# Float32 attention premix in four array quarters and postmix in two halves, two groups of rows at a time

## Chip, cores, metric

One core of a Trainium2 chip runs the whole program in one launch. The metric is the time of one execution in microseconds of the device; the median of the runs counts. The array's clock has two levels, 1.2 and 2.4 GHz; the profile gives the granted share of the higher one.

## What is computed

Twelve-head attention over two batches of 448 rows (head size 64) with two mixing matrices between the heads, then two pairs of dense layers on its 896 x 768 result:

```
scores = scale * matmul(q, k.T)
scores = einsum('bhij,hg->bgij', scores, w_pre)
attn = softmax(scores, axis=-1)        # sum + 1e-09 below
attn = einsum('bhij,hg->bgij', attn, w_post)
x = matmul(attn, v)                    # to 896 x 768
x = moe(x, w_in, w_out)                # h * clip(h + 3, 0, 6) / 6 between
out = moe2(x, w_in, w_out, a, b)       # a cubic over a quadratic in h between
```

All inputs are float32 (the layer weights arrive as 64-bit words whose halves the kernel puts together).

## The kernel before

The kernel has an attention stage and a stage of the dense layers. This case is about the first.

**Chunks and groups.** `plan` cuts each batch's 448 query rows into four chunks, of 120, 120, 120 and 88 rows. A chunk is cut into groups of GR = 10 rows: 12, 12, 12 and 9 of them, 90 in all (m = 0 to 89). For one group the 10 rows times 12 heads are laid on 120 partitions, so that mixing the heads is one product with a 120 x 120 block-diagonal matrix.

**Scores.** `scores(C, hp)` makes the scores of two heads of a chunk: three float32r products (high times high, low times high, high times low) of 64 rows each, one head in the upper and one in the lower 64 rows of the array, into two PSUM banks `sc`. Two copies (L273), one on ScalarE and one on VectorE, move the banks to a staging tile, and DMAs on SP's queue (`spread`, L251) lay it out over the partitions of `full[C]` by row and head. There are two `full` buffers: chunk C+1 is filled while chunk C is used. `k_prep` and `q_prep` split k and q into a high and a low float32r part, the high one on ScalarE and the low one on VectorE.

**A group.** `gsplit` (L293, L295, on GpSimd) splits a group of `full` into `sh` and `sl`. `premix` (L305 to L307) runs three float32r products over the whole array into a bank `M`, VectorE takes the row maximum (L309), ScalarE the exponent with its sum (L311). `norm` (L319, L320) makes the reciprocal of the sum on VectorE, `weigh` (L324, ScalarE) multiplies the block-diagonal postmix matrix `wq` by it into `wr`. `postmix` (L340) has four float32 products, one for each 112 of the 448 columns, with `e` as weights and `wr` as the moving operand, into a bank `A`; an evacuation (L347, some on VectorE) puts it into `at`. The postmix of group m - 2 stands behind the premix of group m. A float32 product appears in the trace as two records, each with a weight load of its own.

**Values.** `av_unit` (L362) multiplies `at` by v for two heads of a chunk, eight float32 products of 64 output columns that alternate between the left and the right half of the array, into a bank `X`; `av_evac` splits the result into the float32r input of the dense layers.

**The order** is written by hand in the loop over chunks and groups: a step is one group; the score pairs of the next chunk stand at steps 1, 3, 5 (two pairs each; 0, 2, 4 in a chunk of 9 groups), the value units of the chunk before at steps 7, 9, 11 (5, 7, 8). Chunk 0 has no value units, and its first scores and those of half of chunk 1 are made ahead of it. In the last chunk (7) the steps also carry the first pieces of the dense layers' weights: `to_f32` on ScalarE and VectorE (L434 to L442) and the split `wh`, `wl` on GpSimd (L458, L459), and the first products `h`.

**PSUM.** Eight banks: two `M`, two `A`, four `sc` (which also serve `X`).

Of the kernel before, what the change touches and what calls it, by code (L numbers as in the profile page):

```python
# [7 lines left out]
F32 = mybir.dt.float32  # L8
# [13 lines left out]
GR = 10  # L22
# [24 lines left out]

@with_exitstack
def fused_kernel(
# [30 lines left out]
    wp_h = const.tile([GP, GR, H], F32R, name="wp_h")  # L80
    wp_l = const.tile([GP, GR, H], F32R, name="wp_l")
    wq = const.tile([GP, H, GR], F32, name="wq")
    mask = const.tile([GP, GR], F32, name="mask")
    wrep = const.tile([GP, 2, H], F32, name="wrep")
# [10 lines left out]
    PRE2 = list(range(2, 12))  # L95
    dram = ctx.enter_context(tc.tile_pool(name="dram", bufs=1, space=bass.MemoryType.DRAM))
# [8 lines left out]
    wtmp = front.tile([GP, GR, H], F32, name="wtmp")  # L105
# [32 lines left out]
    def load_vs():  # L138

        C = len(chunks) - 1  # L140
        t = att.tile([JP, NP, 2, JC * D], F32, tag="full", bufs=2, name="vlast")
# [8 lines left out]
    pw = ps.tile([128, 512], F32, tag="A", name="warm_ps")  # L150
# [9 lines left out]
    for i, w in enumerate((w_pre, w_post)):  # L160
        nc.sync.dma_start(
            out=wrep[:, i, :], in_=w[None, :, :].to_broadcast([GR, H, H])
        )
    load_q(1)
    nc.scalar.preload_act_table_set("natural_log_exp_and_others")
    nc.gpsimd.memset(mask, 1.0)
    nc.gpsimd.affine_select(out=mask, in_=mask, pattern=[[-H, GR]], compare_op=ALU.is_ge,
                            fill=0.0, base=0, channel_multiplier=1)
    nc.gpsimd.affine_select(out=mask, in_=mask, pattern=[[H, GR]], compare_op=ALU.is_ge,
                            fill=0.0, base=H - 1, channel_multiplier=-1)  # L170
# [13 lines left out]
    def build_mix():  # L184
        nc.gpsimd.tensor_tensor(
            out=wtmp,
            in0=mask[:, :, None].to_broadcast([GP, GR, H]),
            in1=wrep[:, 0, None, :].to_broadcast([GP, GR, H]),
            op=ALU.mult,
        )  # L190
        nc.gpsimd.tensor_scalar(out=wtmp, in0=wtmp, scalar1=float(D) ** -0.5, scalar2=None, op0=ALU.mult)
# [805 lines left out]
```

## Time and profile before

| what | value |
|---|---|
| median of 3 runs | 707.35 us (706.45 to 708.13) |
| profiled execution, its own time | 706.12 us |
| span of the profiled execution | 704.4 us |
| granted clock of the array | 0.999 of full speed |
| PE busy | 692.8 us, 98% of the span |
| PEld (weight loads) busy | 618.4 us, 88% |
| DVE (VectorE) busy | 557.1 us, 79% |
| ACT (ScalarE) busy | 411.4 us, 58% |
| POOL (GpSimd) busy | 257.2 us, 37% |
| DMA | 122.81 MB, mean 174 GB/s |

Times in the rows are microseconds from the span's start unless marked ns. A matmul's record begins when it is dispatched and ends when its result stands in PSUM, so records of neighbours overlap: what a matmul costs the array is the distance from one record's start to the next one's, and not its length. The first record after a pause includes the load of its weights. A row marked "x8" merges eight instructions that follow each other.

### The profile page before, as it was taken

To read this page: it belongs to the slowest core of one execution; us is meant where nothing else is said; L and a number is where in the kernel's file an instruction comes from. 1 tells how busy PE (TensorE), PEld (TensorE's weight loads), DVE (VectorE), ACT (ScalarE), POOL (GpSimd) and SP (SyncE) were. 2 spreads that over 40 slices of the span, in tenths; PEclk is the share of its full clock that TensorE was granted. 3 is DMA by queue.
4 is the path that set the end of the run, shared out by engine and by line. 5 is a ranking of instruction groups with operands and counts; after the bars stand their busy time and mean duration, and the time that the engine had idled before them with its cause. 6 is when DMAs were issued, how large, how long until landed. Compare 5 with 4: busy or idle time off the path is not lost.

```text
span 704.4 us, 12410 instructions
## 1 busy us (share of the span) xinstructions
PE 692.8 (98%) x4461; PEld 618.4 (88%) x4461; DVE 557.1 (79%) x934; ACT 411.4 (58%) x851; POOL 257.2 (37%) x255
## 2 busy tenths in 40 slices
PE   8999999999999999999999999999999999999997
PEld 4779888888889888889888888888999999999997
DVE  6855585665567699989998777879999889989991
ACT  6777787787887434434422221247766667669851
POOL 2886775887776333432344454400000000000000
PEclk9999999999999999999999999999999999999999
DMA  6646476545393544454355555367666474755522
GB/s 200 231 135 175 150 202 196 155 140 169 118 262 110 169 130 147 141 169 147 127 171 163 166 187 161 100 241 269 204 243 218 169 264 158 241 184 202 190 80 89
DMA packets 76033, 122.81 MB, mean 174 GB/s; under 512 B 6805, under 2 KB 56261, under 8 KB 75973
## 3 DMA queue, kind: packets, MB, share of 16 engines
q1 hardware_dynamic: 75684, 121.66, 54.2%
q8 instruction: 35, 0.57, 0.3%
q10 hardware_dynamic: 288, 0.37, 0.1%
q14 instruction: 26, 0.20, 0.1%
HBM read 83.39 MB, written 19.27 MB: 146 GB/s over the span
## 4 chain that ended last, share of the span: by engine, by line
PE 60%; DVE 26%; DMA 5%; issue 4%; ACT 3%; POOL 0%; ACTq 0%; POOLq 0%; DVEq 0%
PE A L340 9%; DVE wf L438 6%; DVE wf L442 6%; PE h L388 6%; PE h L387 6%; PE h L386 6%; PE acc L388 6%; PE acc L386 6%; PE acc L387 6%; PE X L362 5%; PE sc L270 4%; DMA pre<-wf 4%; DVE gl L565 4%; DVE wf L436 3%; PE M L305 3%
## 5 line engine op out<-in xcount | busy, mean ns | idle before, releaser
L388 PE MATMUL h<-xh,wl 128*128 128x512 f32 (+1 forms) x384 | 140.7, 366 | 0.9 <-DVE wl L462 0.9
L386 PE MATMUL h<-xh,wh 128*128 128x512 f32 (+1 forms) x384 | 141.1, 367 | 0.0
L387 PE MATMUL h<-xl,wh 128*128 128x512 f32 (+1 forms) x384 | 140.7, 366 | 0.0
L434 ACT ACTIVATE wf<-wraw 128x768 f32<-128x768 f32 (+1 forms) x56 | 48.8, 881 | 92.9 <-DMA pre<-wf 55.1
L295 POOL TENSOR_TENSOR sl<-full,sh 120x448 fp32r<-120x448 f32 x87 | 100.1, 1151 | 7.3
L309 DVE TENSOR_REDUCE st<-M 120x1 f32<-120x448 f32 x90 | 56.0, 623 | 51.1 <-PE M L307 50.6
L340 PEld LDWEIGHTS A<-wr,e 120*112 120x112 f32 x720 | 86.4, 176 | 8.1 <-ACT wr L324 4.0
L340 PE MATMUL A<-wr,e 120*112 120x120 f32 x720 | 88.9, 266 | 2.2 <-ACT wr L324 2.2
L458 POOL TENSOR_SCALAR wh<-wf 128x768 fp32r<-128x768 f32 (+1 forms) x34 | 32.6, 959 | 139.5 <-DVE wf L442 134.8
L311 ACT ACTIVATE e<-M,st 120x448 f32<-120x448 f32 x90 | 57.2, 635 | 40.5 <-DVE st L309 35.4
L388 PEld LDWEIGHTS h<-xh,wl 128*128 128x128 f32 x384 | 72.2, 188 | 9.8 <-DVE wl L462 1.2
L386 PEld LDWEIGHTS h<-xh,wh 128*128 128x128 f32 x384 | 72.2, 188 | 8.0
L387 PEld LDWEIGHTS h<-xl,wh 128*128 128x128 f32 x384 | 72.2, 188 | 7.8
L388 PE MATMUL y<-gh,wl 128*128 128x384 f32 x192 | 70.8, 369 | 0.1
L386 PE MATMUL y<-gh,wh 128*128 128x384 f32 x192 | 70.5, 367 | 0.0
L293 POOL TENSOR_SCALAR sh<-full 120x448 fp32r<-120x448 f32 x87 | 53.9, 619 | 44.0 <-PE M L306 19.5
L387 PE MATMUL y<-gl,wh 128*128 128x384 f32 x192 | 69.9, 364 | 0.0
L459 POOL TENSOR_TENSOR wl<-wf,wh 128x768 fp32r<-128x768 f32 (+1 forms) x34 | 67.7, 1992 | 2.8
L438 DVE SCALAR_TENSOR_TENSOR wf<-wraw,icst,wf 128x768 int32<-128x768 int32 (+1 forms) x56 | 61.7, 1103 | 0.7
L436 DVE TENSOR_SCALAR wf<-wf 128x768 int32<-128x768 int32 x66 | 42.5, 644 | 21.8 <-ACT wf L434 21.5
L442 DVE SCALAR_TENSOR_TENSOR wf<-wraw,icst,wf 128x768 int32<-128x768 int32 (+1 forms) x56 | 57.7, 1032 | 0.6
L564 ACT ACTIVATE gh<-g 128x384 fp32r<-128x384 f32 (+1 forms) x32 | 18.6, 580 | 60.5 <-DVE g L562 60.2
(114 smaller groups left out, 1522.2 us busy)
## 6 DMA issues: line engine op xcount, KB each, us to landing
wraw<-in_moe_w_out_dram SPq DMA_DIRECT2D x28, 768.0 KB
wraw<-in_moe_w_in_dram SPq DMA_DIRECT2D x22, 768.0 KB
full<-stg SPq DMA_DIRECT2D x60, 210.0 KB
vraw<-in_v_dram SPq DMA_DIRECT2D x42, 224.0 KB
wpre<-in_moe_w_in_dram SPq DMA_DIRECT2D x10, 768.0 KB
w2h<-wh SPq DMA_DIRECT2D x16, 384.0 KB
w2l<-wl SPq DMA_DIRECT2D x16, 384.0 KB
ws<-w2h SPq DMA_DIRECT2D x16, 384.0 KB
```

The costliest lines, as they stand in the source:

```text
L293: eng.tensor_scalar(out=sh[:r], in0=s[:r], scalar1=1.0, scalar2=0.0, op0=ALU.mult, op1=ALU.add)
L295: return lambda: eng.tensor_tensor(out=sl[:r], in0=s[:r], in1=sh[:r].bitcast(F32), op=ALU.subtract)
L309: nc.vector.tensor_reduce(out=st[:r, 0:1], in_=mt[:r, :S], op=ALU.max, axis=AX.X, negate=True)
L311: nc.scalar.activation(out=e[:r], in_=mt[:r, :S], func=AF.Exp, bias=st[:r, 0:1], accum_out=st[:r, 1:2])
L340: nc.tensor.matmul(av[:, jc], lhsT=e[:r, jc * JP : (jc + 1) * JP], rhs=wr[:r, :, :rr], start=True, stop=True)
L386: nc.tensor.matmul(o, lhsT=wh, rhs=mh, start=first, stop=False)
L387: nc.tensor.matmul(o, lhsT=wh, rhs=ml, start=False, stop=False)
L388: nc.tensor.matmul(o, lhsT=wl, rhs=mh, start=False, stop=last)
L436: nc.vector.tensor_scalar(out=wi, in0=wi, scalar1=3, scalar2=None, op0=ALU.logical_shift_left)
L438: nc.vector.scalar_tensor_tensor(out=wi, in0=hw, scalar=icst[:, 0:1], in1=wi, op0=ALU.bitwise_and, op1=ALU.bitwise_or)
L442: nc.vector.scalar_tensor_tensor(out=wi, in0=lw, scalar=icst[:, 1:2], in1=wi, op0=ALU.logical_shift_right, op1=ALU.bitwise_or)
L459: nc.gpsimd.tensor_tensor(out=lv, in0=w, in1=hv.bitcast(F32), op=ALU.subtract)
```

## The change

It touches the attention stage alone; the dense layers are the same.

Groups of chunks 1 to 7 are taken two at a time: a chunk of 12 groups has 6 steps, one of 9 has 5, the last of them with a single group. `full` has 128 partitions, and a head of a group row lies at partition 13 i + h (`part_of`; one that would fall on 128 lies at 64), so that five rows of a group lie in either half of 64 partitions; the unused partitions are zeroed once. The premix of two groups is four float32 products of 64 x 64 (`wph` in both halves): half x of the rows, and column half i for group i, into bank `M[x]`. The split on GpSimd (`gsplit`) is gone. The exponents of bank x hold five rows of both groups. The postmix (L357) takes partitions 0 to 59 for the first group and 64 to 123 for the second: 16 float32 products of 60 rows and 60 columns for two groups, in alternation in the upper and the lower half of the array, into two banks `A`. A single group in these chunks has one float32 premix of 128 rows (`wpf`), and chunk 0 keeps groups one at a time on 120 partitions, with one float32 premix (L306).

PSUM is now four `M`, two `A`, two `sc`. `weigh` runs on GpSimd (L319), and the normalization and the weights of a step's groups are made at the start of the next step, ahead of the premix. Both copies of a score pair are on VectorE (L276). The low parts of q (from chunk 3 on) and of the second batch's k are on GpSimd. A step has up to two places for units, "a" right behind the premix and "b" behind the postmix: score pairs at 0a, 0b, 1a, 1b, 2a, 2b in a chunk of 6 steps (0a, 0b, 1a, 1b, 2a, 3a of 5), value units at "b" of the last three steps, two in each. The postmix is that of two steps before; in the last chunk that of one step before, and there each step advances the weight pieces twice. The mixing matrices come laid out from the host side and are loaded instead of being built.

The core of the diff:

```diff
+HR = GR // 2
+HS = H + 1
+NQ = HR * H
+
+
+def part_of(i, h):
+
+    p = HS * i + h
+    return p if p < 128 else 64
...
+    BUFS = {"M": 4, "A": 2, "sc": 2}
...
+    full = [att.tile([128, MG, S], F32, tag=f"full{i}", bufs=1, name=f"full{i}") for i in range(2)] * NCH
+    nc.gpsimd.memset(full[1], 0.0)
...
+    def scores(C, hp, tags=("sc", "sc"), st=None, first=nc.vector.tensor_copy,
                second=nc.vector.tensor_copy):
...
+    def soft_max(e, x):
+        n, st, mt = e["n"], e["st"], e["M"][x]
+        nc.vector.tensor_reduce(out=st[:n, x : x + 1], in_=mt[:n, :S], op=ALU.max, axis=AX.X, negate=True)
+        t = att.tile([128, S], F32, tag="e", bufs=6, name=f"e{e['id']}_{x}")
+        nc.scalar.activation(out=t[:n], in_=mt[:n, :S], func=AF.Exp, bias=st[:n, x : x + 1],
+                             accum_out=st[:n, 2 + x : 3 + x])
+        e["e"].append(t)
+
+    def premix(C, gs):
+
+        e = {"C": C, "gs": gs, "id": f"{C}_{gs[0]}", "n": 128 if C else GP, "e": [], "wr": []}
+        M = e["M"] = [ps.tile([128, 512], F32, tag="M", bufs=BUFS["M"], name=f"M{e['id']}_{x}")
+                      for x in range(len(gs))]
+        s = full[C]
+        if len(gs) == 2:
+            for x in range(2):
+                o = slice(64 * x, 64 * x + 64)
+                for i, g in enumerate(gs):
+                    nc.tensor.matmul(M[x][64 * i : 64 * i + 64, :S], lhsT=wph[o], rhs=s[o, g], start=True, stop=True)
...
+            n, w = e["n"], wpf if C else wp0
+            nc.tensor.matmul(M[0][:n, :S], lhsT=w, rhs=s[:n, gs[0]], start=True, stop=True)
+        e["st"] = att.tile([128, 4], F32, tag="st", bufs=5, name=f"st{e['id']}")
+        entries.append(e)
+        return e
+
+    def weigh(e):
+        n, st, w = e["n"], e["st"], wqh if e["C"] else wq0
+        for x in range(len(e["M"])):
+            c = st[:n, 2 + x : 3 + x]
+            nc.vector.tensor_scalar(out=c, in0=c, scalar1=1e-9, scalar2=None, op0=ALU.add)
+            nc.vector.reciprocal(out=c, in_=c)
+            t = att.tile([128, GP], F32, tag="wr", bufs=6, name=f"wr{e['id']}_{x}")
+            t = t[:n, : w.shape[1] * w.shape[2]].rearrange("p (h i) -> p h i", h=H)
+            nc.gpsimd.tensor_scalar(out=t, in0=w[:n], scalar1=c, scalar2=None, op0=ALU.mult)
+            e["wr"].append(t)
...
+    def postmix(e, byv=False):
+        drain()
+        C, gs = e["C"], e["gs"]
+        if gs[0] == 0:
             at[C] = att.tile([JP, JC, H, CH], F32, tag="at", bufs=2, name=f"at{C}")
...
+        if not C:
+            A = bank(0)
+            for jc in range(JC):
+                nc.tensor.matmul(cols(A, GR)[:, jc], lhsT=e["e"][0][:GP, jc * JP : (jc + 1) * JP], rhs=e["wr"][0],
+                                 start=True, stop=True)
+            take(A, rows[0], GR, byv)
+            return
+        n = HR * len(gs)
+        A = [bank(r) for r in range(2)]
+        for x in range(len(gs)):
+            for jc in range(JC):
+                for r in range(2):
+                    o = slice(64 * r, 64 * r + NQ)
+                    nc.tensor.matmul(
+                        cols(A[r], n)[:, jc, :, x * HR : x * HR + HR], lhsT=e["e"][x][o, jc * JP : (jc + 1) * JP],
+                        rhs=e["wr"][x][o], start=True, stop=True
+                    )
+        for r in range(2):
+            take(A[r], rows[r] if len(gs) == 2 else rows[0] + r * HR, n, byv and r)
 
...
+    PRE, VAT = B * NCH - 2, 11
+    BYV = {0: (5, 7, 9), 6: (4, 5), 5: (4,)}
...
+                sched.setdefault((kind, steps[i * len(steps) // len(units)]), []).append(u)
+
+        if not C:
+            add("b", [lambda h=h: scores(1, h) for h in range(FIRST, NP)], [1, 3, 5])
+            add("p", [lambda: q_prep(2, 0, NP // 2), lambda: q_prep(2, NP // 2, NP)], [7, 8])
+        elif nxt is not None:
+            for h, w in zip(range(NP), (0, 1, 2, 3, 4, 5) if NS == 6 else (0, 1, 2, 3, 4, 6)):
+                add("ab"[w % 2], [lambda h=h: scores(nxt, h)], [w // 2])
+            if C + 2 < len(chunks):
+                add("p", [lambda: q_prep(C + 2, 0, NP // 2, nc.gpsimd), lambda: q_prep(C + 2, NP // 2, NP, nc.gpsimd)],
+                    [4, 5] if NS == 6 else [4])
+        if C:
+            add("b", [lambda h=h: av_unit(C - 1, h) for h in range(1, H, 2)],
+                [1, 2, 3] if nxt is None else [3, 4, 5] if NS == 6 else [2, 3, 4])
...
+            if entries and not entries[-1]["wr"]:
+                weigh(entries[-1])
+            for p in xposts:
                 p[0]()
...
+            room(BUFS["sc"] + 1)
+            e = premix(C, gs)
+            if ("a", s) in sched:
                 low()
...
+            do("a", s)
+            soft_max(e, 0)
+            room(BUFS["sc"] + 1)
+            if len(gs) == 2:
+                soft_max(e, 1)
+            low()
+            do("p", s)
+            do("k", s)
             for p in preps:
-                p[0]()
-            lows[:] = preps
+                for x in p:
+                    x()
             preps.clear()
...
+            if C > PRE or (C == PRE and s == NS - 1):
+                for _ in range(1 + (C > PRE)):
+                    next(wpieces, None)
+            while len(entries) > (2 if nxt is not None else 1):
+                postmix(entries.pop(0), s in BYV[NS if C else 0])
+            do("b", s)
```

**VectorE in chunk 4, steps with scores.** `sc5_n` are the score banks of chunk 5, `st` the maxima and sums, `M46` group 46's premix, `M4_2_1` bank 1 of the pair that begins with group 2 of chunk 4. Before:

```order
L309 TENSOR_REDUCE st47_1926<-M47_1922 120x1
L273 COPY stg5_1_1902<-sc5_3_1901 120x448
L309 TENSOR_REDUCE st48_1949<-M48_1945 120x1
L319 TENSOR_SCALAR st47_1926<-st47_1926 120x1
L320 RECIPROCAL st47_1926<-st47_1926 120x1
L319 TENSOR_SCALAR st48_1949<-st48_1949 120x1
L320 RECIPROCAL st48_1949<-st48_1949 120x1
```

Now, one whole step:

```order
L276 COPY stg5_1_1741<-sc5_2_1739 120x448
L276 COPY stg5_1_1741<-sc5_3_1740 120x448
L287 TENSOR_REDUCE st4_2_1768<-M4_2_0_1762 128x1
L276 COPY stg5_2_1771<-sc5_4_1769 120x448
L276 COPY stg5_2_1771<-sc5_5_1770 120x448
L287 TENSOR_REDUCE st4_2_1768<-M4_2_1_1763 128x1
L315 TENSOR_SCALAR st4_2_1768<-st4_2_1768 128x1
L316 RECIPROCAL st4_2_1768<-st4_2_1768 128x1
L315 TENSOR_SCALAR st4_2_1768<-st4_2_1768 128x1
L316 RECIPROCAL st4_2_1768<-st4_2_1768 128x1
L276 COPY stg5_3_1800<-sc5_6_1798 120x448
L276 COPY stg5_3_1800<-sc5_7_1799 120x448
```

Four score copies stand in one step where one stood between two maxima, and the normalization of a step's second bank stands between that bank's maximum and the next copies.

**GpSimd in the last chunk, now.** `wr7_2_0` are the postmix weights of bank 0 of the pair that begins with group 2 of chunk 7, `wh` and `wl` the split of a unit of layer weights.

```order
L319 TENSOR_SCALAR wr7_0_0_2960<-wq_59,st7_0_2900 128x60
L319 TENSOR_SCALAR wr7_0_1_2964<-wq_59,st7_0_2900 128x60
L473 TENSOR_SCALAR wh_2981<-wf_2842 128x768
L474 TENSOR_TENSOR wl_2982<-wf_2842,wh_2981 128x768
L319 TENSOR_SCALAR wr7_2_0_3031<-wq_59,st7_2_2972 128x60
L319 TENSOR_SCALAR wr7_2_1_3035<-wq_59,st7_2_2972 128x60
```

The postmix weights, on ScalarE before, now stand on GpSimd's queue behind a unit's split.

## Rows read from the trace of the kernel before

**Rows 1.** Page, part 1: busy time, share of the span, instructions.
```profile
PE 692.8 (98%) x4461; PEld 618.4 (88%) x4461; DVE 557.1 (79%) x934; ACT 411.4 (58%) x851; POOL 257.2 (37%) x255
```

**Rows 2.** Windows: stretch, length, busy PE, PEld, DVE, ACT, POOL; clock, DMA share, GB/s.
```profile
160.00:180.00 20.00, 20.00 (x204) 17.87 (x203) 10.37 (x33) 14.97 (x42) 14.07 (x17) 1.00 0.48 145
240.00:260.00 20.00, 20.00 (x100) 17.84 (x99) 17.20 (x18) 7.98 (x12) 9.05 (x6) 1.00 0.54 167
```

**Rows 3.** Chain that ended last, 20 to 235 us, by line.
```profile
by line: PE A L340 28.9%; PE X L362 16.2%; PE sc L270 12.0%; PE M L305 10.3%; PE M L307 7.4%; PE M L306 6.9%; DMA vraw<-in_v_dram 2.8%; issue 2.5%; DVE st L309 1.6%; ACT wf L434 1.2%; POOL sl L295 1.1%; DMA full<-stg 1.0%; ACT e L311 0.8%; 
```

**Rows 4.** Timeline of PE: first premix of chunks 0, 1, 5, 6, 7; first dense product.
```profile
15.45 0.44 PE L305 MATMUL M<-sh,wp_h 120*120 120x448 f32 x1 [0.16 <-DVE sh L293]
...
37.68 0.47 PE L305 MATMUL M<-sh,wp_h 120*120 120x448 f32 x1 [0.73 <-POOL sh L293]
...
146.64 0.46 PE L305 MATMUL M<-sh,wp_h 120*120 120x448 f32 x1
...
174.56 0.46 PE L305 MATMUL M<-sh,wp_h 120*120 120x448 f32 x1
...
202.39 0.46 PE L305 MATMUL M<-sh,wp_h 120*120 120x448 f32 x1
...
221.01 0.42 PE L386 MATMUL h<-xh,wh 128*128 128x384 f32 x1
```

**Rows 5.** Timeline of PE in chunk 5: scores, two groups, scores.
```profile
150.60 0.37 PE L270 MATMUL sc<-xh,ql 64*120 64x448 f32 x2
150.80 0.36 PE L270 MATMUL sc<-xh,qr 64*120 64x448 f32 x2
...
151.40 0.36 PE L306 MATMUL M<-sh,wp_l 120*120 120x448 f32 x1
151.60 0.37 PE L307 MATMUL M<-sl,wp_h 120*120 120x448 f32 x1
...
152.83 0.36 PE L306 MATMUL M<-sh,wp_l 120*120 120x448 f32 x1
...
153.24 0.98 PE L340 MATMUL A<-wr,e 120*112 120x120 f32 x8
154.15 0.47 PE L270 MATMUL sc<-xh,qr 64*120 64x448 f32 x2
154.45 0.37 PE L270 MATMUL sc<-xh,ql 64*120 64x448 f32 x2
```

**Rows 6.** Value units: two in the timeline; records starting in 108.84 to 108.95.
```profile
113.68 1.86 PE L362 MATMUL X<-at,vraw 112*64 112x120 f32 x32
...
L362 PE MATMUL X<-at,vraw x2: 317/317/317, 108.8 to 108.8; 112*64 112x120 f32 x2
```

**Rows 7.** Timeline of PEld: loads of a group's first two premix products.
```profile
112.06 0.18 PEld L305 LDWEIGHTS M<-sh,wp_h 120*120 120x120 f32 x1
112.16 0.18 PEld L306 LDWEIGHTS M<-sh,wp_l 120*120 120x120 f32 x1
```

**Rows 8.** Timeline: two copies, an exponent, the two normalization steps behind it.
```profile
12.78 1.15 DVE L273 COPY stg<-sc 120x448 f32<-120x448 f32 x2
...
149.69 0.63 ACT L311 ACTIVATE e<-M,st 120x448 f32<-120x448 f32 x1 [0.30 <-DVE st L319]
150.22 0.19 ACT L311 ACTIVATION_READ_ACCUMULATOR e<-M,st 120x1 f32 x1
...
150.45 0.15 DVE L319 TENSOR_SCALAR st<-st 120x1 f32<-120x1 f32 x1 [0.59 <-ACT e L311]
150.64 0.16 DVE L320 RECIPROCAL st<-st 120x1 f32<-120x1 f32 x1
150.74 0.62 DVE L273 COPY stg<-sc 120x448 f32<-120x448 f32 x1
```

**Rows 9.** Page, part 5: costliest groups (busy us, mean ns | idle before).
```profile
L295 POOL TENSOR_TENSOR sl<-full,sh 120x448 fp32r<-120x448 f32 x87 | 100.1, 1151 | 7.3
L309 DVE TENSOR_REDUCE st<-M 120x1 f32<-120x448 f32 x90 | 56.0, 623 | 51.1 <-PE M L307 50.6
...
L458 POOL TENSOR_SCALAR wh<-wf 128x768 fp32r<-128x768 f32 (+1 forms) x34 | 32.6, 959 | 139.5 <-DVE wf L442 134.8
...
L459 POOL TENSOR_TENSOR wl<-wf,wh 128x768 fp32r<-128x768 f32 (+1 forms) x34 | 67.7, 1992 | 2.8
```

More of the change, by code (lines that the diff above doesn't have):

```diff
@@ L501, in fused_kernel @@
             flush()
-        scores(0, hp, (("M", "A"), ("sc", "sc"))[hp % 2], stage[:, 2 * hp : 2 * hp + 2],
-               second=nc.scalar.copy if hp == NP - 2 else nc.vector.tensor_copy)
+        scores(0, hp, ("M", "sc", "M", "A", "M", "sc")[hp : hp + 1] * 2, stage[:, 2 * hp : 2 * hp + 2],
+               first=nc.scalar.copy, second=nc.scalar.copy if hp == NP - 2 else nc.vector.tensor_copy)
         flush()
+    scale_pre(wp0)
     for g in range(chunks[0][3]):
@@ L586, in fused_kernel, with add @@
         nxt = C + 1 if C + 1 < len(chunks) else None
+        groups = [[g] for g in range(G)] if not C else [list(range(g, min(g + 2, G))) for g in range(0, G, 2)]
+        NS = len(groups)
         sched = {}
-        def add(units, steps):
+        def add(kind, units, steps):
             for i, u in enumerate(units):
-                sched.setdefault(steps[i * len(steps) // len(units)], []).append(u)
-        sst = SST[G] if C else ONES
-        if nxt is not None:
-            kw = {} if C else {"first": nc.vector.tensor_copy}
-            add([lambda h=h: scores(nxt, h, **kw) for h in range(0 if C else FIRST, NP)], sst)
@@ L602, in fused_kernel @@
         if C == NCH - 1:
-            add([lambda h=h: k_prep(1, h) for h in range(4, NP)], [0, 1])
-        if C > 0:
-            add([lambda h=h: av_unit(C - 1, h) for h in range(1, H, 2)], [("av", a) for a in (AVST[G] if nxt is not None else AVLAST)])
-        for s in range(G):
-            if s == (5 if C == 1 else 0) and C and C + 2 < len(chunks):
+            add("k", [lambda h=h: k_prep(1, h, nc.gpsimd) for h in range(2, NP)], [0, 0, 1, 1])
+        if C == PRE:
+            add("p", [lambda c=c: x_move(c, 0, XEAR) for c in range(3)], [3, 4, 5])
@@ L609, in fused_kernel, with do, low @@
+        if C > PRE:
+            add("p", [lambda c=c: x_move(c, 0, XEAR) for c in range(3, KD)], [0, 1, 2])
+            add("p", [lambda: x_move(slice(0, KD), XEAR, XRAW)], [2])
+        def do(*key):
+            for u in sched.get(key, []):
+                u()
+        def low():
+            for p in xposts:
+                p[1]()
+            xposts.clear()
+        for s, gs in enumerate(groups):
+            if s == (2 if C == 1 else 0) and C and C + 2 < len(chunks):
                 load_q(C + 2)
@@ L685, in pieces @@
         for _ in range(n):
-            next(wpieces)
-    drain()
-    norm(m - 1)
+            next(wpieces, None)
+    weigh(entries[0])
     flush()
-    postmix(m - 2)
     run(h100)
-    weigh(m - 1)
     h110 = gemm1(1, 0, ps.tile([128, 512], F32, tag="sc", bufs=BUFS["sc"], name="h1_1_0"))
     next(h110)
-    postmix(m - 1)
+    postmix(entries.pop())
     for _ in range(2):
@@ L715, in fused_kernel @@
     pieces(2)
[L716 removed]
+    run(gemm1(1, 1, ps.tile([128, 512], F32, tag="M", bufs=BUFS["M"], name="h1_1_1")))
     load_units(4)
```

252 lines of the change are left out of this document (78 added, 174 removed).

## Prediction

> **What bounds the kernel now.** I read the busy shares first: the array (PE) is busy for 98% of the span [rows 1], and the windows grant it the higher of its two clocks (1.00, [rows 2]). They also split the busy time by stage: in the attention (160 to 180 us) PE and in the dense layers (240 to 260 us) PE again are busy for the whole 20 us, while VectorE has 10.4 and ScalarE 15.0 us of work in the first. A busy share can hide waits, so next I read the chain over the attention [rows 3]: its entries down to premix, scores, values and postmix are all PE's, some 82% together, and the rest are single waits of 1 to 3%. So the attention is a queue of array work, and I check that by adding it up. One group's premix and postmix take 1.43 us (from one second premix product to the next, 151.40 to 152.83); a 448-column float32r product takes 0.20 [rows 5]. That leaves 0.83 for the eight postmix records, 0.103 each; a record of a float32 product passes its 120 columns twice, so a column costs 0.43 ns. A score pair is three rounds of 0.20 (150.60 to 150.80), 0.60 us. Of the value units' records the first two start together, and the 32 of two units take 1.86 us with the last one's tail [rows 6]: two run at a time, 8 x 0.103 = 0.82 a unit. A change between whole array, row halves and column halves costs 0.19: the postmix that began at 153.24 fills 0.82, to 154.06, and the scores' first round counts from 154.25 (0.20 ahead of the second, 154.45) [rows 5].
>
> A chunk of 12 groups has thus 12 x 1.43 + 6 x 0.60 + 6 x 0.82 + 12 changes x 0.19 = 17.2 + 3.6 + 4.9 + 2.3 = 28.0 us. Chunk 5 takes 27.92 (146.64 to 174.56) and chunk 6 27.83 [rows 4]. The array bounds this stage; whatever else is slow there is hidden.
>
> **Premix, removed and added.** Two groups have six products of 0.20, 1.2 us. Now they have four float32 products of two records each, 896 column passes per record: 0.385 at 0.43 ns, 0.77 for both. If all four quarters run at once a pair costs 0.77. No row shows four at a time; rows 5 show two row halves at once, rows 6 two column halves at once. Bounds: 0.77 (all at once) to 1.54 (two by two). I take 0.77, because in [rows 6] the float32 products already overlap from the first record on with different moving data. The split on GpSimd goes (100 us of `sl` alone, [rows 9]); the array waits for it in 1.1% of the chain only [rows 3], so its going gains nothing by itself.
>
> **Postmix.** Two groups had 16 records of 0.103, 1.65 us. Now there are 32 records of 60 columns, two at once: 16 rounds of at least 2 x 60 x 0.43 = 0.052 us. But each record needs its own weights, 112 columns as before. Two loads of 120 columns follow each other by 0.10 [rows 7], so a load of 112 takes 0.093, and it can hide behind one round only. I take 0.097 a round, 1.55 us a pair; bounds 0.052 (loads no limit) to 0.19 (the loads of both halves one behind the other). The Trainium skill, "TensorE: Matmul & The Clock Gate", section "LDWEIGHTS (loading the stationary operand)", speaks against this part: a load's time goes by its columns, P / 1.2 ns, and half the rows save nothing. By that, 16 x 0.093 = 1.49 us a pair would be the least, and rows 7 agree (0.10 for 120); by columns alone it would be 0.84.
>
> **A 12-group chunk on the array.** 6 x (0.77 + 1.55) + 3.6 + 4.9 + changes. The premix has a mode of its own, but scores and postmix share one: two changes in a score step, three in a value step, 15 x 0.19 = 2.9. Sum 25.3 us against 27.9: the gain would be 2.6 a chunk.
>
> **What is late next: VectorE in the score steps.** Both copies of a pair are now VectorE's, four in a step, and with two score banks in place of four the next pair can't start before both are copied. The order shows the loop: two copies 1.15 [rows 8]; the next pair on the array (0.04 to react, 0.10 load, 0.60, tail 0.36 - 0.20 = 0.16, 0.04 to react) 0.94, in which a maximum of 0.62 [rows 9] is hidden; two more copies 1.07 up to the next start; the second maximum 0.62; ScalarE's exponent with its sum, 149.69 to 150.41, 0.72, with 0.04 on either side; the normalization up to the next copy, 150.45 to 150.74, 0.29 [rows 8]. Together 4.87 us. The array needs 0.77 + 1.55 + 1.20 + 0.38 = 3.90 in such a step. The first score step of a chunk has no copies in front and keeps 3.9; the second and third lose 0.97 each, the first value step 0.2. 25.3 + 2.1 = 27.4, a gain of 0.5 in each of chunks 1, 2, 4, 5 and 6: **-2.5 us**. Bounds: the loop doesn't close (-13) or each hop costs 0.1 more (+3).
>
> **Chunk 3** (9 groups): 9 x 1.43 + 3.6 + 4.9 + 2.3 = 23.7 before; now 4 x 2.32 + 0.77 + 0.78 + 3.6 + 4.9 + 13 x 0.19 = 21.8, and 2.2 for the loop: 24.0, **+0.3** (bounds -2 and +1.5).
>
> **Chunk 0** took 22.2 us (15.45 to 37.68, [rows 4]). Its premix costs 0.77 for 0.60. The normalization of a group now stands ahead of the next group's maximum, which closes a loop: maximum 0.62, exponent 0.72, normalization 0.29, 0.08 to react, 1.71 a group. 12 x 1.71 = 20.5; three score pairs with two changes, 1.0 each; two splits of q in the loop, at the price of the copy as nearest row, 0.6 each: 24.7, **+2.5** (bounds: 12 x 0.17 = +2 for the array alone, and +4).
>
> **Chunk 7.** The postmix follows its premix by one step, and its weights stand on GpSimd behind a unit's split in two steps: 0.96 + 1.99 = 2.95 [rows 9]. They are wanted about a premix and a change later, and VectorE's part lies in between; I estimate 1.2 lost each time. The first step has two postmixes, and the second needs both `A` banks emptied: two evacuations, at 0.6 each as the copies, with a quarter hidden: 0.9. **+3.3** (bounds 0 and 7).
>
> **Edits at nothing.** `weigh` off ScalarE, which has slack of 5 in 20 us [rows 2] (if the exponent were late it would show in the loops above). Loads of the mixing matrices, the zeroing of `full[1]` on GpSimd and of the gaps by two DMAs on SP's queue ahead of chunk 2's spreads, one more spread DMA per chunk: SP's spreads have over a chunk's half before they are needed; the zeroing runs while the first k is awaited (if it outlasts that, one product's low part is late, up to +2). The low parts of q and k on GpSimd come steps before use. The dense layers are unchanged and bound by the array, so the sum passes through whole.
>
> **Sum.** -2.5 + 0.3 + 2.5 + 3.3 = +3.6 us. The profiled execution took 706.12, which is 1.2 below the median shown; 709.7 on its scale, **711.0 us** against the median of 707.35. A measurement of this kernel tells about 0.2% (1.4 us) from no change.
>
> **Rivals.**
>
> *Quarters two by two.* A pair's premix costs 1.54. In score steps the loop hides it (3.90 + 0.77 is below 4.87), in the 15 value steps of the five long chunks and four of chunks 3 and 7 it does not: 19 x 0.77 = +14.6, 725.6; half of that, 718, if the second row half starts one record late. For it: no row has four at once. Against: the overlap of rows 6. Chance 0.18.
>
> *Records in strict order.* If the second record of a quarter blocks the first of the next, a pair takes five records of 0.385 in a staircase, 1.93: 19 x 1.16 = 22, and 0.2 in the ten score steps: 735. The Trainium skill, the same page, section "The mechanism" in Part 3, says that matmuls start strictly in program order. Rows 6 speak against it: by that order the first record would start alone, and two start together. Chance 0.03.
>
> *Not slower: the loads don't set the pace.* If a round of the postmix takes 0.052, a pair saves 0.72 in 24 steps that the array bounds (19 and the first score steps), 17 us: 694; at 0.075, 702. For it: nothing in the trace shows a stream of loads as the limit. Against: rows 7. It decides below 0.085 us a round. Chance 0.20.
>
> *Loads one behind the other.* 16 x 0.19 = 3.1 a pair, 1.5 more in 38 pairs, less 10 in the score steps: +47, 758. Chance 0.03.
>
> *As forecast:* 0.56, with 706 to 716 from the bounds of chunks 0 and 7 and of the loops.
>
> **Numbers.** Slower: 0.48 of the forecast's 0.56, the two premix rivals and the serial loads, 0.72, rounded to 0.70. Faster: 0.17 of the third rival and 0.03 of the forecast, 0.20. Same: 0.10. The range takes in the forecast, the quarters two by two up to 726 and the upper part of the faster rival from 702.
>
> **What would show it.** Premix of two groups: eight records that span about 0.8 us and, at first, four starts together. Postmix records two by two, 0.097 apart, with PEld busy throughout. In score steps PE idle of about 1 us before `sc`, released by VectorE's copy, and steps 4.9 us apart. Chunk 5 near 27.4 us, chunk 0 near 24.7, the last chunk near 22. I am wrong if value steps take over 5 us (array rivals) or under 4 (loads), or if the score steps come at 3.9.

## The result, and the profile after

The changed kernel takes 712.30 us (median of nine executions, 708.63 to 714.11), the kernel before 706.67 beside it (704.71 to 709.02): ratio **1.0074, 95% interval 1.0054 to 1.0094**. The forecast was 711.0, slower. The direction came true. So did the size, but in part by luck: two terms of the sum were wrong by several us, and they largely cancel.

The profiled execution is the quickest of the nine: 708.63 us, span 706.5, against 706.12 and 704.4 of the one shown of before. The page after, its busy shares [rows 1] and the granted clock in 40 slices (all 9 in the profiled execution of the kernel before):

```profile
PE 686.8 (97%) x5147; PEld 586.0 (83%) x5147; DVE 562.1 (80%) x962; ACT 364.3 (52%) x713; POOL 164.6 (23%) x182
...
PEclk9999999999998999999999999999999999999999
```

In the clock line the 8 stands in the slice from 212 to 230 us, the last chunk. The array's timeline in chunk 5, first a premix, then two score steps (columns: start, us, engine, line, operation, records):

```profile
147.33 0.98 PE L303 MATMUL M<-full,wp 64*64 64x448 f32 x8
148.24 0.46 PE L273 MATMUL sc<-xh,qr 64*120 64x448 f32 x2
...
148.94 1.69 PE L357 MATMUL A<-wr,e 60*112 60x60 f32 x32
150.45 0.44 PE L273 MATMUL sc<-xh,qr 64*120 64x448 f32 x2
...
151.23 0.98 PE L303 MATMUL M<-full,wp 64*64 64x448 f32 x8
152.67 0.99 PE L273 MATMUL sc<-xh,qr 64*120 64x448 f32 x2 [0.46 <-DVE stg L276]
...
156.19 0.98 PE L303 MATMUL M<-full,wp 64*64 64x448 f32 x8
```

Eight premix records fill 0.98 us with their tail, and the next product comes 0.91 after their start (147.33 to 148.24): 0.72, if a change costs 0.19 as in the kernel before. The first records of all four products start within 0.02 us of each other. So four quarters do run at once (0.77 forecast). The 32 postmix records take 1.51 us (148.94 to 150.45), 16 rounds of 0.094, and the weight loads are busy for 1.50 of these 1.51 us. The first score step lasts 3.90 us, the second 4.96, and in the second the array waits for VectorE's copy. The waits of the weight loads from 15 to 235 us (us in total, times, longest), where most of that waiting is booked:

```profile
PEld sc L273 <- DVE stg L276: 17.4, 25, 1.3
PEld A L347 <- POOL wr L319: 9.7, 10, 2.0
PEld A L357 <- POOL wr L319: 9.4, 13, 1.0
```

The last chunk shows what no step of the forecast had (timeline of PE):

```profile
203.26 0.40 PE L357 MATMUL A<-wr,e 60*112 60x60 f32 x2
204.34 1.78 PE L357 MATMUL A<-wr,e 60*112 60x60 f32 x30 [0.68 <-ACT at L342]
206.94 2.15 PE L357 MATMUL A<-wr,e 60*112 60x60 f32 x32 [0.83 <-ACT at L342]
209.02 1.36 PE L303 MATMUL M<-full,wp 64*64 64x448 f32 x8
210.30 3.24 PE L357 MATMUL A<-wr,e 60*112 60x60 f32 x32
213.48 3.23 PE L377 MATMUL X<-at,vraw 112*64 112x120 f32 x32
216.63 0.98 PE L303 MATMUL M<-full,wp 64*64 64x448 f32 x8
```

The windows of the same stretch (length, busy PE, PEld, DVE, ACT, POOL; clock, DMA share, GB/s):

```profile
205.00:210.00 5.00, 4.17 (x62) 3.10 (x59) 1.90 (x6) 3.29 (x9) 0.83 (x2) 0.95 1.06 267
210.00:215.00 5.00, 5.00 (x52) 4.59 (x50) 2.52 (x7) 3.63 (x8) 2.29 (x2) 0.50 0.23 57
215.00:220.00 5.00, 5.00 (x74) 4.07 (x72) 2.25 (x5) 1.93 (x6) 1.17 (x3) 0.87 0.55 170
```

Behind two waits for ScalarE the clock falls to the lower level for some 7 us (0.5 + 5 + 1.3 by the three means; 0.50 is 1.2 GHz); 32 postmix records take 3.24 us there for 1.78, 32 value records 3.23 for 1.86. The granted mean of this execution is 0.995, that of the other eight 0.988 to 0.990.

Where the time went, in us, from the starts of each chunk's first premix, of the first dense product behind the last value products, and the span's end (the right columns are experiments below):

| stretch | before | after | e0_again | e1_copies | e3_fill | e5_after_pad | e11_best |
|---|---|---|---|---|---|---|---|
| to chunk 0 | 15.45 | 15.91 | 16.03 | 16.20 | 16.06 | 16.11 | 16.11 |
| chunk 0 | 22.23 | 25.51 | 25.53 | 25.54 | 25.53 | 25.52 | 24.60 |
| chunks 1 to 6 | 164.71 | 160.93 | 160.94 | 154.04 | 160.91 | 160.95 | 154.35 |
| last chunk and tail | 30.44 | 36.38 | 38.25 | 38.35 | 35.14 | 39.76 | 35.03 |
| dense layers | 471.57 | 467.77 | 467.45 | 467.27 | 467.06 | 470.86 | 467.81 |
| span | 704.4 | 706.5 | 708.2 | 701.4 | 704.7 | 713.2 | 697.9 |

Two lines are news: the last chunk loses 5.9 us (7.8 in the second profile of the same kernel), and the dense layers, of which no instruction was changed, gain 3.8.

### The profile page after: what moved, and what is told of

It reads as the page before. It is cut to its first block, busy times and chain, and to the rows that moved or that the text cites. A ratio compares the mean times of both kernels' runs of the same rounds, so it can differ in the third digit from the quotient of the medians.

```text
span 706.5 us, 13542 instructions
## 1 busy us (share of the span) xinstructions
PE 686.8 (97%) x5147; PEld 586.0 (83%) x5147; DVE 562.1 (80%) x962; ACT 364.3 (52%) x713; POOL 164.6 (23%) x182
## 4 chain that ended last, share of the span: by engine, by line
PE 54%; DVE 27%; DMA 8%; ACT 5%; issue 4%; POOL 1%; SPq 0%; DVEq 0%; ACTq 0%; POOLq 0%
PE A L357 6%; DVE wf L453 6%; PE h L403 6%; PE acc L401 6%; PE acc L403 6%; PE h L402 6%; PE acc L402 6%; PE h L401 5%; DVE wf L457 5%; PE X L377 5%; DMA pre<-wf 4%; DVE stg L276 3%; DVE gl L577 3%; PE sc L273 3%; PE M L303 3%
## 5 line engine op out<-in xcount | busy, mean ns | idle before, releaser
L401 PE MATMUL h<-xh,wh 128*128 128x512 f32 (+1 forms) x384 | 139.5, 363 | 0.0
L289 ACT ACTIVATE e<-M,st 128x448 f32<-128x448 f32 (+1 forms) x90 | 56.7, 632 | 86.3 <-DVE st L287 62.9
L357 PEld LDWEIGHTS A<-wr,e 60*112 60x112 f32 x1248 | 72.2, 178 | 19.0 <-POOL wr L319 9.4
L287 DVE TENSOR_REDUCE st<-M 128x1 f32<-128x448 f32 (+1 forms) x90 | 53.9, 616 | 31.8 <-PE M L303 25.4
L357 PE MATMUL A<-wr,e 60*112 60x60 f32 x1248 | 75.2, 262 | 2.4 <-ACT at L342 1.5
L319 POOL TENSOR_SCALAR wr<-wq,st 128x60 f32<-128x60 f32 (+1 forms) x90 | 41.4, 466 | 121.0 <-DVE st L316 63.7
L451 DVE TENSOR_SCALAR wf<-wf 128x768 int32<-128x768 int32 x66 | 42.2, 640 | 25.2 <-ACT wf L449 24.9
L273 PE MATMUL sc<-xh,qr 64*120 64x448 f32 (+1 forms) x192 | 49.6, 401 | 7.0 <-DVE stg L276 4.9
L273 PEld LDWEIGHTS sc<-xh,qr 64*120 64x120 f32 (+1 forms) x192 | 25.5, 172 | 29.9 <-DVE stg L276 17.4
```

The source lines that it names most:

```text
L273: mm = nc.tensor.matmul(sc[i][:n, :S], lhsT=w[o, hp, :n], rhs=x[o], start=(j == 0), stop=(j == 2))
L287: nc.vector.tensor_reduce(out=st[:n, x : x + 1], in_=mt[:n, :S], op=ALU.max, axis=AX.X, negate=True)
L289: nc.scalar.activation(out=t[:n], in_=mt[:n, :S], func=AF.Exp, bias=st[:n, x : x + 1], accum_out=st[:n, 2 + x : 3 + x])
L357: nc.tensor.matmul(cols(A[r], n)[:, jc, :, x * HR : x * HR + HR], lhsT=e["e"][x][o, jc * JP : (jc + 1) * JP], rhs=e["wr"][x][o], start=Tru ...
L401: nc.tensor.matmul(o, lhsT=wh, rhs=mh, start=first, stop=False)
L451: nc.vector.tensor_scalar(out=wi, in0=wi, scalar1=3, scalar2=None, op0=ALU.logical_shift_left)
```

## Experiments

All are edits of the changed kernel unless said otherwise. Ratios are to the kernel before on the same chip.

**The changed kernel again** (no edit).

> The changed kernel once more, unedited. Its profiled execution took 708.63 us, the fastest of nine (median 712.30), with a mean granted clock of 0.995; the other eight show 0.988 to 0.990. Theory A (the clock): the stretch at half clock that the profile shows in the last chunk (0.50 from 210 to 215 us) is in every execution, and is longer in most: at a mean of 0.990 over 710 us it would be 0.010 x 710 / 0.5 = 14 us long and cost 7, at 0.995 half of that. Then the ratio is 1.006 to 1.009 again and a profile with 0.990 has some 14 us at half clock at one place in the last chunk. Rival B (loops): the loss is VectorE's and GpSimd's loops of the forecast, in all executions alike, and the half clock is one profile's accident: then this profile has a full clock from 195 to 235 us and the last attention product still ends about 6 us later than in the kernel before.

Measured: 711.81 us, ratio 1.0061 (1.0036 to 1.0086), mean clock 0.988 to 0.992 in its executions. The windows:

```profile
200.00:205.00 5.00, 4.05 (x61) 2.99 (x60) 2.71 (x9) 3.55 (x9) 1.02 (x3) 1.00 1.06 345
205.00:210.00 5.00, 4.17 (x66) 3.79 (x68) 2.33 (x7) 3.27 (x9) 0.84 (x2) 0.92 1.06 287
210.00:215.00 5.00, 5.00 (x46) 3.53 (x40) 2.52 (x7) 3.19 (x8) 1.21 (x2) 0.50 0.17 46
215.00:220.00 5.00, 5.00 (x49) 3.39 (x46) 0.27 (x1) 1.25 (x3) 2.25 (x3) 0.56 0.33 89
```

Some 10 us at the lower level (0.8 + 5 + 4.4), at the same place. Theory A holds: the fall is the kernel's own, and longer in most executions than in the one profiled first.

**Score copies: one engine each again.**

```diff
-    def scores(..., first=nc.vector.tensor_copy,
+    def scores(..., first=nc.scalar.copy,
```

> In the score steps of chunks 1 on, the first copy of a score pair goes back to ScalarE, the second stays on VectorE. My theory (VectorE's loop of 4.87 us sets the second and third score step of a chunk): 0.97 us each for ten steps, 17.4 us of weight-load waits behind VectorE's copies in all; with two copies side by side the loop falls to 3.8 us, under the array's 3.9, so these waits go, a 12-group chunk takes about 25.5 instead of 27.4, and the kernel is 8 to 10 us faster than the changed one: ratio to the kernel before 0.994 to 0.997. Rival (the array or ScalarE sets these steps anyway: ScalarE then has copies and exponents in turn): waits for the copies go to waits for the exponents, and the ratio stays within 0.3% of the changed kernel's, 1.004 to 1.010.

Measured: 704.84 us, ratio **0.9950 (0.9922 to 0.9978)**, 7.0 us below the changed kernel, and significantly below the kernel before. Chunks 1 to 6 take 154.0 us for 160.9. In chunk 5 the second score step is 4.33 us for 4.96 (PE's timeline):

```profile
143.61 0.98 PE L303 MATMUL M<-full,wp 64*64 64x448 f32 x8
...
147.51 0.98 PE L303 MATMUL M<-full,wp 64*64 64x448 f32 x8
148.84 0.47 PE L273 MATMUL sc<-xh,qr 64*120 64x448 f32 x2 [0.34 <-ACT stg L276]
...
151.84 0.98 PE L303 MATMUL M<-full,wp 64*64 64x448 f32 x8
```

VectorE's loop was what ate the array's gain. The gain is 1 us under the expected 8 to 10, since the loop now closes over ScalarE's copy (12.3 us of load waits for it) at 4.33 and not at 3.9.

**Chunk 0: the multiplication back on ScalarE.**

```diff
-            nc.gpsimd.tensor_scalar(out=t, in0=w[:n], scalar1=c, scalar2=None, op0=ALU.mult)
+            if e["C"]:
+                nc.gpsimd.tensor_scalar(out=t, in0=w[:n], scalar1=c, scalar2=None, op0=ALU.mult)
+            else:
+                nc.scalar.activation(out=t, in_=w[:n], func=AF.Copy, scale=c)
```

> In chunk 0 alone the postmix weights are multiplied on ScalarE again, as in the kernel before, and not on GpSimd. Chunk 0 took 25.5 us against 22.2. Theory G: GpSimd's multiplication (0.47 us, and its waits: 9.7 us of weight loads wait for it in chunk 0, up to 2.0 at once) holds the postmix; then chunk 0 falls by 2 us or more, ratio 1.003 to 1.005. Rival L (the forecast's term): the loop of maximum, exponent and normalization on VectorE and ScalarE, 1.71 us a group, sets chunk 0; ScalarE's multiplication of about 0.25 joins that engine's work, chunk 0 stays between 25 and 27 us and the ratio between 1.006 and 1.010.

Measured: 711.20 us, 1.0052 (1.0031 to 1.0074), not to be told from the changed kernel. Chunk 0 takes 25.11 us (16.54 to 41.65), as rival L had it, and the wait has only another name (the load waits of 15 to 41 us):

```profile
PEld A L350 <- ACT wr L322: 9.2, 10, 2.0
```

GpSimd isn't what holds chunk 0.

**Ten idle products in the last chunk's first step.**

```diff
             while len(entries) > (2 if nxt is not None else 1):
+                if nxt is None and s == 0:
+                    pf = ps.tile([128, 512], F32, tag="sc", bufs=BUFS["sc"], name=f"fill{len(entries)}")
+                    for i in range(5):
+                        nc.tensor.matmul(pf, lhsT=wf16[:, :128], rhs=wf16, start=(i == 0), stop=(i == 4))
                 postmix(entries.pop(0), s in BYV[NS if C else 0])
```

(`wf16` is a 128 x 512 bfloat16 tile of zeros.)

> In the first step of the last chunk five idle products of 512 columns (of zeros, read by nobody) stand ahead of each of the two postmixes, where TensorE waited 0.68 and 0.83 us for ScalarE to empty the banks. Theory A: the clock falls to half at about 210 us behind a stretch in which TensorE waits (4.3 and 4.2 of 5 us busy from 200 to 210); with the waits filled it stays full, and 3.5 us (by the profile with 0.995) to 7 us (by 0.990) come back, less up to 1 us for what the fill adds: ratio 0.999 to 1.004, mean clock 0.998 or more. Rival C (the clock answers to something else there, such as the kind of work in the whole chunk, or it costs nothing because the last chunk waits anyway): the clock stays at 0.990 to 0.995, the ratio at 1.006 to 1.010.

Measured: 707.12 us, ratio **0.9992 (0.9974 to 1.0010)**, mean clock 0.998 to 1.000 in ten executions. The windows:

```profile
205.00:210.00 5.00, 4.65 (x67) 3.78 (x67) 2.34 (x7) 3.27 (x9) 0.84 (x2) 1.00 1.07 252
210.00:215.00 5.00, 5.00 (x79) 3.90 (x80) 2.53 (x7) 4.20 (x10) 1.62 (x2) 1.00 0.42 103
```

Work that nobody reads makes the kernel 4.7 us faster than its unedited runs on the same chip (711.81), as much as the loss against the kernel before. That the lower clock cost about this much is shown: the same 32 postmix records take 1.78 us at 1.00 and 3.24 at 0.50. Whether the filled waits keep it up or the kind of work that fills them is not: the fill changes both. A wait alone doesn't bring the clock down: in this run the array waits 0.86 us for weights later in the same chunk, at a clock of 1.00, and in chunk 0 of the changed kernel 1.31 us, at 1.00 too.

**The place of the dense tiles, in the kernel before.** The pool of constants grew by 384 bytes per partition with the change, so every dense tile stands 384 bytes higher. Here they stand 640 lower:

```diff
-    wp_l = const.tile([GP, GR, H], F32R, name="wp_l")
-    mask = const.tile([GP, GR], F32, name="mask")
-    wrep = const.tile([GP, 2, H], F32, name="wrep")
...
+    wp_l = att.tile([GP, GR, H], F32R, tag="wp_l", bufs=1, name="wp_l")
+    mask = front.tile([GP, GR], F32, name="mask")
+    wrep = front.tile([GP, 2, H], F32, name="wrep")
```

> The kernel before, with three of its small constants (the low premix weights, the mask and the replicated mixing matrices) taken out of the pool of constants into pools that are freed after the attention; nothing else changes, and every tile of the dense layers starts 640 bytes lower. From the end of the last value products on, the changed kernel's dense layers took 467.1 to 467.8 us in five profiles, those of the kernel before 471.6: the 512-column products follow each other by 228.6 ns there for 232.4 here. In the changed kernel the pool of constants is 384 bytes larger, and 384 up and 640 down are the same place in a grid of 1,024. Theory P (place): the spacing goes by where the dense tiles stand in SBUF; then it falls to about 228.6 ns here, the dense layers to about 467.5, and the ratio is 0.993 to 0.996. Rival Q (the instruction stream, or the load that the attention leaves on queues and engines): spacing 232.4 as before, ratio 0.998 to 1.002.

**And back, in the changed kernel:**

```diff
+    pad = const.tile([128, 160], F32, name="pad")
+    nc.gpsimd.memset(pad, 0.0)
```

> The changed kernel with 640 unused bytes more in the pool of constants, so that the dense tiles stand 1,024 bytes above their places in the kernel before. Theory P: the 512-column products are 232.4 ns apart again, the dense layers take about 471.5 us, and the ratio rises from about 1.007 to 1.011 to 1.014. Rival Q: nothing changes, 228.6 ns and 1.005 to 1.009.

Eighteen 512-column products in the second dense pair, from the first to the next product behind them (PE's timeline), first the kernel before:

```profile
560.12 0.39 PE L386 MATMUL h<-xh,wh 128*128 128x512 f32 x1
...
564.31 0.34 PE L386 MATMUL acc<-wh,g0h 128*128 128x384 f32 x1
```

The changed kernel:

```profile
563.54 0.39 PE L401 MATMUL h<-xh,wh 128*128 128x512 f32 x1
...
567.66 0.33 PE L401 MATMUL acc<-wh,g0h 128*128 128x384 f32 x1
```

The kernel before, moved:

```profile
565.11 0.39 PE L386 MATMUL h<-xh,wh 128*128 128x512 f32 x1
...
569.23 0.33 PE L386 MATMUL acc<-wh,g0h 128*128 128x384 f32 x1
```

The changed kernel, padded:

```profile
569.21 0.39 PE L403 MATMUL h<-xh,wh 128*128 128x512 f32 x1
...
573.40 0.34 PE L403 MATMUL acc<-wh,g0h 128*128 128x384 f32 x1
```

4.19, 4.12, 4.12 and 4.19 us: the pace goes with the place, in both kernels and both directions, as theory P had it. In the kernel with the ten idle products, whose zeros add 1,024 bytes per partition to the same pool, the eighteen take 4.12 too (561.76 to 565.88). The padded kernel takes 715.34 us, ratio 1.0110 (1.0093 to 1.0127), and its dense layers 470.9 us for 467.5. The moved kernel before takes 705.38, 0.9981 (0.9955 to 1.0007), which tells nothing by itself and is above the 0.993 to 0.996 expected. Its five executions with a mean clock of 0.999 or more have a median of 704.3, the twelve such of the kernel before beside it 706.4; that choice of executions was made afterwards. Its dense layers took 471.1 us in the profiled execution in spite of the quicker products, with load waits in the products into `y` (waits from 245 us on), where the kernel before has 0.7 us of them for GpSimd:

```profile
PEld y L388 <- POOL wl L459: 3.1, 5, 1.0
PEld y L387 <- DVE gl L565: 1.1, 1, 1.1
```

So there most of the gain became a wait for weight splits. Which property of the place counts stays open; only these places were tried.

This profiled execution, 710.14 us, is the slowest of its ten, and it shows the lower clock in the layout of the kernel before as well. At the start of chunk 1 the array waits 2.85 us for GpSimd's split, and then this follows (windows):

```profile
40.00:45.00 5.00, 4.80 (x17) 3.94 (x18) 1.06 (x4) 1.52 (x4) 4.75 (x7) 0.50 0.09 31
```

So a fall of the clock isn't peculiar to quarter- and half-array products. The kernel before itself has mean clocks from 0.993 to 1.000 in its executions.

**Chunk 0: the normalization behind the next maximum.**

```diff
-            if entries and not entries[-1]["wr"]:
+            if C and entries and not entries[-1]["wr"]:
                 weigh(entries[-1])
...
             soft_max(e, 0)
+            if not C and len(entries) > 1:
+                weigh(entries[-2])
```

> In chunk 0 the normalization of the group before stands behind this group's maximum on VectorE again, as in the kernel before; GpSimd still multiplies. Forecast's term: the loop of maximum, exponent and normalization, 1.71 us a group, makes chunk 0's 25.5 us; with the exponent under the next maximum the loop is gone, and chunk 0 falls to 22.5 to 23.5 us, the ratio by 0.003 to 0.004, to 1.003 to 1.005. Rival (copies of scores and the splits of q on VectorE hold chunk 0, not the order of the normalization): chunk 0 stays over 24.8 us and the ratio at 1.006 to 1.009.

Measured: 710.17 us, 1.0030 (1.0012 to 1.0047), and chunk 0 takes 25.68 us (15.92 to 41.60): a miss, with chunk 0 where the rival had it. A group without score copies comes down from 1.83 to 1.67 us, but another wait stands in (VectorE's timeline), the staging tile still being read:

```profile
29.05 1.16 DVE L276 COPY stg<-sc 120x448 f32<-120x448 f32 x2 [1.32 <-DMA full<-stg]
```

The small gain in the ratio isn't clear of noise (its interval overlaps that of the unedited kernel's second run), and it isn't chunk 0's; chunk 1's first step is 0.6 us shorter (3.82 for 4.41).

**Last chunk: one postmix a step.**

```diff
-                [1, 2, 3] if nxt is None else [3, 4, 5] if NS == 6 else [2, 3, 4])
+                [2, 3, 4] if nxt is None else [3, 4, 5] if NS == 6 else [2, 3, 4])
...
-            while len(entries) > (2 if nxt is not None else 1):
+            while len(entries) > 2:
...
-    weigh(entries[0])
+    weigh(entries[-1])
     flush()
+    postmix(entries.pop(0))
     run(h100)
```

> In the last chunk the postmix keeps its distance of two steps, so that no step has two postmixes; the chunk before's value units come a step later, and one postmix more is left for the tail. Theory A (waits bring the clock down): the waits of 0.68 and 0.83 us for ScalarE at 204 and 206 us and those for GpSimd's weights go, the clock stays full, and the end of the attention falls from 240.7 to 234 to 236 us: ratio 0.998 to 1.001. Rival C (the clock falls with the work of the chunk, whatever waits): half clock for 6 to 10 us again near 210 us, of the 7 us only the 1.5 to 3 of the waits come back, ratio 1.002 to 1.006.

Measured: 711.25 us, 1.0054 (1.0027 to 1.0080), in the range of rival C. Three of ten executions keep a clock of 1.000 and take 707.3 to 708.9; the others have 0.988 to 0.995 and take 710.9 to 716.2. One wait is left, and in the profiled execution the clock falls right behind it, while the array is busy throughout:

```profile
204.62 1.78 PE L357 MATMUL A<-wr,e 60*112 60x60 f32 x30 [0.80 <-ACT at L342]
206.33 1.65 PE L303 MATMUL M<-full,wp 64*64 64x448 f32 x8
207.91 3.24 PE L357 MATMUL A<-wr,e 60*112 60x60 f32 x32
```

So the clock falls without the double postmix too. That the missing wait is what spared three executions is likely, and not shown.

**The first weight piece later.** The wait that is left has a cause that the trace of the first repeat names (ScalarE's timeline): a weight conversion that waits for its load, with the emptying of the banks behind it.

```profile
203.35 0.89 ACT L449 ACTIVATE wf<-wraw 128x768 f32<-128x768 f32 x1 [1.43 <-DMA wraw<-in_moe_w_in_dram]
204.14 0.57 ACT L342 ACTIVATE at<-A 112x480 f32<-112x480 f32 x1
```

```diff
-            if C > PRE or (C == PRE and s == NS - 1):
-                for _ in range(1 + (C > PRE)):
+            if C > PRE:
+                for _ in range(2):
```

> The first piece of the first weight unit (ScalarE's conversion, which at 201.9 us waits 1.2 us for the unit's load, with the emptying of the postmix's banks queued behind it) goes from the last step of the chunk before into the last chunk; the rest is the changed kernel. Theory W (the load, not the two postmixes, makes the two waits of 0.7 and 0.8 us at 204 and 206 us, and with them the clock falls): ScalarE empties the banks by 203, both waits shrink to under 0.4 us together, the clock stays full or falls only in some executions, and the ratio is 0.999 to 1.003. Rival D (two postmixes in one step wait for their own banks whatever stands on ScalarE): the second wait stays at 0.8 us, half clock for 6 to 10 us again, ratio 1.005 to 1.008.

Measured: 714.13 us, 1.0096 (1.0064 to 1.0129): slower in the median than the changed kernel (1.0061 in its second run), but the intervals overlap. The first wait goes; the second grows, since the conversion now stands ahead of the next emptying (PE's timeline):

```profile
203.41 1.78 PE L357 MATMUL A<-wr,e 60*112 60x60 f32 x32
207.60 3.43 PE L357 MATMUL A<-wr,e 60*112 60x60 f32 x32 [2.40 <-ACT at L342]
```

W was wrong about the second wait: 2.40 us in one piece replace 0.95 + 0.83, and the clock falls again.

**Together.** Copies, normalization and piece:

> The first score copy on ScalarE, chunk 0's normalization behind the next maximum, and the first weight piece later, all three. If the three act apart, their gains on the changed kernel add: 7.0 us (copies) + 1.6 (normalization; 0.003 of 708) + 0 to 5 (piece, mostly by the clock): 5 to 9 us below the kernel before, ratio 0.987 to 0.993. Rival (they share one slack, or ScalarE, which now has copies, exponents and conversions, becomes late in the last chunk): no more than the copies alone gave, 0.994 to 0.997.

Measured: 708.30 us, 1.0013 (0.9992 to 1.0034), clock 0.983 to 0.992: outside both expectations, worse than the copies alone. The wait of 2.40 us is there too, and both windows from 200 to 210 us show a clock of 0.50.

The same with the ten idle products:

> The same three, and the ten idle products in the first step of the last chunk. Where the clock of the run before this one is full without them, they only cost: up to 2.5 us of TensorE's time, ratio 0.002 to 0.004 above it. Where it still falls to half for some us, they give 3 to 5 us back: mean clock 0.999 or more in every execution and a ratio of 0.985 to 0.989.

Measured: 702.10 us, **0.9923 (0.9896 to 0.9951)**, clock 0.995 to 1.000, 6.2 us below the run before it. The idle products give even more where the wait was longer, but ratio and clock stay short of the expected ones.

And without the moved piece:

> The first score copy on ScalarE, chunk 0's normalization behind the next maximum, and the ten idle products; the first weight piece stays where the change put it, since moving it later cost 2.3 us (714.1 for 711.8). If that price holds here too: 702.1 - 2.3 = 699.8 us on the scale of the last runs, ratio 0.987 to 0.991. Rival (with the idle products in, TensorE is busy through that step either way, and the piece's place costs nothing): the ratio stays at 0.992 and above.

Measured: 699.36 us, **0.9887 (0.9849 to 0.9924)**: as expected, and the lowest ratio of all runs. Its interval overlaps that of the run before it, so the piece's own price here isn't settled. Its page, and a window of the last chunk in which the array waits 1.27 us for GpSimd's weights and the clock stays at 1.00:

```profile
PE 680.6 (98%) x5157; PEld 582.3 (83%) x5157; DVE 544.2 (78%) x923; ACT 381.5 (55%) x752; POOL 165.2 (24%) x183
...
205.00:210.00 5.00, 3.73 (x62) 2.79 (x62) 3.23 (x10) 4.65 (x12) 3.46 (x4) 1.00 0.54 161
```

## Why the prediction was right, and where it was wrong

**Right: the array's terms.** Four quarters run at once, 0.72 for 0.77, and the postmix is paced by its loads, 0.094 a round for 0.097. A pair's postmix took 1.65 us before and takes 1.51 now, so half the rows bought little. By the rule cited from the Trainium skill, "TensorE: Matmul & The Clock Gate", section "LDWEIGHTS (loading the stationary operand)", a load of 112 columns takes 0.093, an estimate. This trace agrees with it (0.094). The rival of records in strict order would have had 1.93 us for a premix; the trace speaks against it with 0.72 and the four starts together. The Trainium skill, the same page, section "The mechanism" in Part 3, which was named beside that rival, is about the order in which matmuls start and end. That a second record holds up the next product was the prediction's reading of it.

**Right: what is late next.** The loop of 4.87 us was measured as 4.96 and 4.78 (151.23, 156.19, 160.97), the first score step as 3.90 for 3.9, and undoing the copies gave 7.0 us back. The five long chunks gained 3.4 us for 2.5 forecast (1.5, 0.4, 0.7, 0.7 and 0.0, and not 0.5 each); chunk 3 gained 0.4 where 0.3 was to be lost.

**Right in its loop, too low for the splits: chunk 0.** It took +3.3 us for +2.5. The forecast's loop stands in VectorE's timeline of the changed kernel (four maxima and one low part of q):

```profile
21.36 0.62 DVE L287 TENSOR_REDUCE st<-M 120x1 f32<-120x448 f32 x1
...
23.04 0.60 DVE L287 TENSOR_REDUCE st<-M 120x1 f32<-120x448 f32 x1
...
32.05 0.62 DVE L287 TENSOR_REDUCE st<-M 120x1 f32<-120x448 f32 x1
33.91 0.53 DVE L239 TENSOR_TENSOR ql<-qraw,qr 128x360 fp32r<-128x360 f32 x1 [1.24 <-ACT qr L238]
...
35.19 0.62 DVE L287 TENSOR_REDUCE st<-M 120x1 f32<-120x448 f32 x1
```

From one maximum to the next it takes 1.67 to 1.74 us where nothing else stands between (1.71 forecast), 2.7 to 2.8 with score copies, and 3.14 and 2.58 with the two splits of q. A split thus adds 1.4 and 0.9 where 0.6 was counted: VectorE's low part waits for ScalarE's high part, which stands behind the exponent of the same step, while the kernel before made the low part a step later. But the loop isn't the only limit. With the normalization taken out of it chunk 0 still took 25.7, and neither of the two edits to it saved more than 0.4; with the copies split as well it took 25.3, 24.9 and 24.6 in three runs. No run moved the splits, so their part is read from the trace and not shown by a change.

**Wrong: the last chunk's term of +3.3.** It measured +5.9, of which the lower clock makes some 3.3 in the profiled execution: 1.5 for the postmix (3.24 for 1.78), 1.4 for the value unit, 0.4 for the premix. In the other executions it lasts longer. The rest, 2.6, holds 1.5 of waits for the banks where 0.9 was counted, and 0.6 of the array's waiting for weights where 2.4 was counted (1.9 in the last run above, at full clock). The step that failed is "two evacuations ... 0.9": it priced the wait, and not that ScalarE's conversion would wait for its load ahead of the emptying, nor that the clock, 1.00 in all windows read [rows 2], could fall behind it.

**Wrong: "The dense layers are unchanged and bound by the array, so the sum passes through whole."** They gained 3.8 us through a pool of constants 384 bytes larger. With +0.5 at the start the account of the profiled execution closes: 0.5 + 3.3 - 3.8 + 5.9 - 3.8 = +2.1, the difference of the spans. The median's +5.6 is larger because most executions have more time at the lower clock (a mean of 0.990 for 0.995 is 7 us more of 710 at half the clock, 3.5 lost). That the total came within 1.3 us of the forecast is luck to that extent: the last chunk lost more than forecast, and the dense layers' gain, for which the sum had nothing, made up for it. Without the clock's fall and with the dense tiles' gain the change costs nothing (e3_fill, 0.9992).

## What to carry to other kernels

An array stage that gets cheaper runs into the next loop at once; here splitting the two copies between two engines again was worth more than the whole loss. When a pool changes size, compare the spacing of untouched products before and after, since their place can be worth as much as the edit. And read the granted clock of every stretch and every execution: here a chunk with two waits of 0.7 to 0.8 us lost 3.3 us or more to the clock that fell behind them.

## What the runs showed of the hardware that was not expected

- The pace of 512-column products depends on where their tiles stand in SBUF: 18 of them take 4.19 us where the kernel before has them and 1,024 bytes above, and 4.12 us 384 bytes above and 640 below; an unedited stage lost or gained 3.4 to 3.8 us by it.
- The granted clock fell to the lower level behind waits of 0.7 to 1.0 us in the last chunk of the changed kernel, in both its profiles, and behind one of 2.85 us in the layout of the kernel before. It stayed at 1.00 behind waits of 1.31 us in chunk 0 and, with ten 512-column products on zeros ahead, of 0.86 and 1.27 us in the last chunk. What decides stays open.
- GpSimd's multiplication of 128 x 60 values took 0.45 us on average and that of 120 x 120 0.58: half the columns save only a quarter of the time.
